# Sinkhorn attention followed by a squared-ReLU FFN: TensorE's order written out by hand, the first batch in halves, exp written contiguously

## The chip, the cores and the metric

The kernel runs on one core of one Trainium2 chip. The metric is the device time of one execution in microseconds (us); lower is better. Weights and activations arrive from device memory as float32 and are cast to bfloat16 by the loads; the result is stored as float32.

## The reference

Four batches, eight heads, 768 positions of width 64. A sorting matrix `P` (8 x 8 for each head) is made by five rounds of exp and row and column normalisation. It mixes the eight blocks (96 positions each) of `k` and `v`; each block of `q` then attends to the mixed block of the same number. The result, 3072 tokens of width 512, goes through a two-layer FFN.

```python
for _ in range(5):
    P = P - np.max(P, axis=-1, keepdims=True)
    P = np.exp(P)
    P = P / (np.sum(P, axis=-1, keepdims=True) + 1e-09)
    P = P / (np.sum(P, axis=-2, keepdims=True) + 1e-09)
k_sorted = np.einsum('bhij,bhjcd->bhicd', P, k_b).reshape(B, H, S, D)
v_sorted = np.einsum('bhij,bhjcd->bhicd', P, v_b).reshape(B, H, S, D)
...
scores = scale * np.matmul(q_b, k_sb.transpose(0, 1, 2, 4, 3))
attn = np.exp(scores)   # after subtraction of the row maximum
attn = attn / (np.sum(attn, axis=-1, keepdims=True) + 1e-09)
out = np.matmul(attn, v_sb)
...
h = np.maximum(x @ w_in, 0.0)      # 512 -> 2048
y = h * h @ w_out                  # 2048 -> 512
```

## The kernel before

The kernel is written against a layer that records operations, puts them in an order for each engine by its own priorities, and adds the semaphores. Every engine then executes its own instructions strictly in that order, so an instruction that waits holds up all behind it on its engine.

**Start.** `sort_net` is loaded on SP's queue; ScalarE and VectorE alternate through the five rounds (lines 90 to 112), and eight small matmuls (`pt`, line 117) and five VectorE products (`build_w`, line 127) spread the matrix over `w_all`. All loads of `q`, `k`, `v` and of the weights are issued by GpSimd (POOL, lines 72, 148, 151), which also fills the padding of the work tiles (`sT`, `et`, `vs`, lines 188, 194, 223). POOL is one queue: a fill that stands behind a load whose turn has not come waits with it.

**Attention** works on a pair of heads at a time: `attention(b, hp)`, four pairs in each batch, 16 in all. In order: 12 transposes of `q` (`qtp`, line 162) and a copy to `qT` on VectorE; 12 matmuls for `k` and 12 for `v` (`tp`, line 176), taken out by ScalarE (line 185) and by VectorE (line 187); 16 score matmuls (`scp`, line 200) and four exps on ScalarE (`et`, line 206); 8 transposes of `v` (`vbp`, line 215), copied by VectorE; 16 value matmuls (`oup`, line 231), normalised by VectorE (lines 238 and 239); 8 transposes back (`xtp`, line 247), copied to `xT` (line 251). The exp reads a row of scores contiguously from PSUM, ordered n, a, c, and writes it to `et` ordered n, c, a: neighbours that it reads land 12 bytes apart in SBUF.

**FFN**, `ffn_group(mc)`, works on 512 tokens, six groups in all: 16 steps of four matmuls of 512 columns (`hp`, line 258), each followed by a ReLU on ScalarE (line 264) and a square on VectorE (line 265); then four output tiles of 16 matmuls (`op`, line 270), a copy on ScalarE (line 276) and a store.

PSUM is shared out by pools: `ps1` has one slot (tag `p1`: `qtp`, `vbp`, `xtp`), `ps2` two (tag `p2`: `tp`, `scp`, `oup`), `psf` three (tag `pf`: `hp`, `op`). A slot is free again when its tile has been read out. The main loop runs batch 0's attention, then for each later batch its attention and one or two FFN groups of the batch before; which matmul of the two stands next on TensorE was the recording layer's choice.

Of the kernel before, what the change touches and what calls it, by code (L numbers as in the profile page):

```python
# [8 lines left out]
FP32 = mybir.dt.float32  # L9
# [7 lines left out]
def kernel(  # L17
# [18 lines left out]
    HP = H // 2  # L36
    d_model = moe_w_in.shape[0]
# [4 lines left out]
    MC = n_tok // 512  # L42
# [3 lines left out]
    sink = ctx.enter_context(tc.tile_pool(name="sink", bufs=1))  # L46
    wpool = ctx.enter_context(tc.tile_pool(name="wpool", bufs=1))
# [18 lines left out]
    def load(b, parts):
        n = H // parts
        ts = [ld.tile([128, H, NA * D], BF16, tag=t, name=t) for t in ("qb", "kb", "vb")]
        qkv[b] = ts
        for g in range(parts):  # L70
            for t, src in zip(ts, (q_r, k_r, v_r)):
                nc.gpsimd.dma_start(  # L72
                    out=t[:, n * g:n * (g + 1), :],
                    in_=src[b, :, n * g:n * (g + 1), :])

    ident = const.tile([128, 128], BF16)
    make_identity(nc, ident)
    load(0, 4)
# [34 lines left out]


    pt = ps1.tile([128, NB, NH], FP32, tag="p1")
    for i in range(NB):
        nc.tensor.matmul(
            out=pt[:, i, :],
            lhsT=pb[:, i, :, :].rearrange("h j c -> h (j c)"),
            rhs=ident[0:NH, 0:NH],  # L120
            start=True, stop=True)


    w_all = wpool.tile([128, NH, NB, C0], BF16)

    def build_w(h0, n):
        nc.vector.tensor_tensor(
            out=w_all[:, h0:h0 + n, :, :],
            in0=mask[:, None, None, :].to_broadcast([128, n, NB, C0]),
            in1=pt[:, :, h0:h0 + n].rearrange("p i h -> p h i")[:, :, :, None]  # L130
            .to_broadcast([128, n, NB, C0]),
            op=ALU.mult)

    build_w(0, 2)
    build_w(2, 6)
    for b in range(1, B):
        build_w(8 * b, 8)

    w_in_bf = wpool.tile([128, KC, d_ff], BF16)
    w_out_bf = wpool.tile([128, NT, d_model], BF16)  # L140
    xT = wpool.tile([128, KC, n_tok], BF16)
    w_in_r = moe_w_in.rearrange("(kc p) f -> p kc f", p=128)
    w_out_r = moe_w_out.rearrange("(nt p) m -> p nt m", p=128)

    def load_weights():
        for g in range(2):
            f = slice(d_ff // 2 * g, d_ff // 2 * (g + 1))
            nc.gpsimd.dma_start(out=w_in_bf[:, :, f], in_=w_in_r[:, :, f])
        for g in range(2):
            t = slice(NT // 2 * g, NT // 2 * (g + 1))  # L150
            nc.gpsimd.dma_start(out=w_out_bf[:, t, :], in_=w_out_r[:, t, :])

    def attention(b, hp):
        hA = 2 * hp
        qb, kb, vb = qkv[b]
        w = [w_all[:, 8 * b + hA + e, :, :].rearrange("p i c -> p (i c)") for e in range(2)]


        qtp = ps1.tile([128, NA, 128], BF16, tag="p1")
# [6 lines left out]
        qT = att.tile([128, NB, NA, C0], BF16, tag="qT")
        nc.vector.tensor_copy(  # L167
            out=qT, in_=qtp.rearrange("p a (i c) -> p i a c", c=C0))


        st = []
        for name, src, eng in (("ks", kb, "act"), ("vs", vb, "dve")):
            tp = ps2.tile([128, NA, 128], FP32, tag="p2")
            for a in range(NA):
                for e in range(2):
                    nc.tensor.matmul(  # L176
                        out=tp[64 * e:64 * (e + 1), a, :],
                        lhsT=src[:, hA + e, D * a:D * (a + 1)],
                        rhs=w[e], start=True, stop=True)

            sT = att.tile([128, S + 32], BF16, tag=name + "T")
            view = sT[:, 0:S].rearrange("p (i c a) -> p i c a", c=C0, a=NA)
            tpv = tp.rearrange("p a (i c) -> p i c a", c=C0)
            if eng == "act":
                nc.scalar.copy(out=view, in_=tpv)  # L185
            else:
                nc.vector.tensor_copy(out=view, in_=tpv)  # L187
            nc.gpsimd.memset(sT[:, S:S + 32], 0.0)  # L188
            st.append(sT)
        ksT, vsT = st  # L190


        et = att.tile([96, 2, S + 32], BF16, tag="et")
        nc.gpsimd.memset(et[:, :, S:S + 32], 0.0)  # L194
        for hf in range(2):
            scp = ps2.tile([128, 2, 512], FP32, tag="p2")
            for n in range(4):
                i = 4 * hf + n
# [54 lines left out]
    def ffn_group(mc):  # L253
# [70 lines left out]
```

## Time and profile before

| | us |
|---|---|
| median of 3 runs | 349.79 (349.43 to 349.99) |
| profiled execution, its own time | 349.75 |
| span of the profiled execution, first to last instruction | 348.0 |
| TensorE busy, matmuls | 260.1 |
| ScalarE busy | 168.1 |
| VectorE busy | 119.8 |
| mean granted TensorE clock (1.00 is 2.4 GHz) | 0.882 |

Some 1.75 us of a run lie outside the span. Busy times are unions over an engine's instructions; matmuls are pipelined and their ends are modelled, so the distance between the starts of two pieces of work says more than a matmul's own duration. Times below are counted from the span's start.

### The profile page before, as it was taken

To read this page: it belongs to the slowest core of one execution; us is meant where nothing else is said; L and a number is where in the kernel's file an instruction comes from. 1 tells how busy PE (TensorE), PEld (TensorE's weight loads), DVE (VectorE), ACT (ScalarE), POOL (GpSimd) and SP (SyncE) were. 2 spreads that over 40 slices of the span, in tenths; PEclk is the share of its full clock that TensorE was granted. 3 is DMA by queue.
4 is the path that set the end of the run, shared out by engine and by line. 5 is a ranking of instruction groups with operands and counts; after the bars stand their busy time and mean duration, and the time that the engine had idled before them with its cause. 6 is when DMAs were issued, how large, how long until landed. Compare 5 with 4: busy or idle time off the path is not lost.

```text
span 348.0 us, 5090 instructions
## 1 busy us (share of the span) xinstructions
PE 260.1 (75%) x2083; PEld 138.1 (40%) x2120; DVE 119.8 (34%) x260; ACT 168.1 (48%) x206; POOL 31.9 (9%) x104
## 2 busy tenths in 40 slices
PE   0224566569669598766969999966867899999995
PEld 0123344335335344433534444433534444444442
DVE  5812254246236302533531141143544303402400
ACT  2133643685673515577471362277476315514611
POOL 8812003200004100000000000000000000000000
PEclk9999965688686899888689999988678899999999
DMA  7999961940004931000001200200000021011011
GB/s 101 200 211 207 204 107 21 191 62 2 0 3 52 196 85 62 0 2 0 2 1 44 79 0 33 81 11 0 2 0 2 0 78 45 0 60 62 1 60 60
DMA packets 19430, 20.25 MB, mean 58 GB/s; under 512 B 976, under 2 KB 15312, under 8 KB 19408
## 3 DMA queue, kind: packets, MB, share of 16 engines
q0 software_dynamic: 15904, 13.63, 25.2%
q1 hardware_dynamic: 3504, 6.30, 4.8%
q8 instruction: 16, 0.26, 0.3%
q14 instruction: 6, 0.05, 0.1%
HBM read 27.27 MB, written 6.29 MB: 96 GB/s over the span
## 4 chain that ended last, share of the span: by engine, by line
PE 62%; ACT 21%; issue 8%; DMA 6%; POOL 1%; DVE 1%; ACTq 0%; POOLq 0%
PE op L270 24%; PE hp L258 23%; ACT et L206 17%; PE tp L176 6%; DMA w_in_bf<-in_moe_w_in_dram 4%; PE xtp L247 3%; PE qtp L162 2%; ACT h L264 2%; PE oup L231 2%; DMA kb<-in_k_dram 2%; DVE ao L239 1%; PE scp L200 1%; ACT sT L185 0%; POOL qb L72 0%; POOL vb L72 0%
## 5 line engine op out<-in xcount | busy, mean ns | idle before, releaser
L258 PE MATMUL hp<-xT,w_in_bf 128*128 128x512 bf16 x356 | 102.8, 419 | 3.7 <-issue 3.0
L206 ACT ACTIVATE et<-scp 96x384 bf16<-96x384 f32 x64 | 85.0, 1595 | 20.9 <-PE scp L200 20.8
L270 PE MATMUL op<-w_out_bf,h 128*128 128x512 bf16 x375 | 85.1, 382 | 0.6 <-issue 0.2
L264 ACT ACTIVATE h<-hp 128x512 bf16<-128x512 f32 x96 | 60.0, 627 | 49.1 <-PE hp L258 35.0
L265 DVE TENSOR_TENSOR h<-h 128x512 bf16<-128x512 bf16 x96 | 40.7, 424 | 77.7 <-ACT h L264 77.6
L231 PE MATMUL oup<-vs,et 96*128 96x65 bf16 x256 | 19.2, 220 | 51.7 <-ACT et L206 47.0
L270 PEld LDWEIGHTS <-h 128*128 128x128 bf16 x384 | 37.5, 99 | 44.6 <-issue 0.8
L258 PEld LDWEIGHTS <-w_in_bf 128*128 128x128 bf16 x384 | 36.9, 104 | 42.6 <-issue 11.2
L276 ACT COPY ob<-op 128x512 f32<-128x512 f32 x24 | 14.1, 586 | 71.6 <-PE op L270 68.7
L231 PEld LDWEIGHTS <-et 96*128 96x128 bf16 x256 | 13.3, 113 | 61.9 <-ACT et L206 55.9
L238 DVE RECIPROCAL rec<-oup 96x8 f32<-96x8 f32 x32 | 6.4, 199 | 59.1 <-PE oup L231 59.1
L185 ACT CAST sT<-tp 128x768 bf16<-128x768 f32 x16 | 12.8, 799 | 27.8 <-PE tp L176 27.8
L239 DVE TENSOR_TENSOR ao<-oup,rec 96x512 bf16<-96x512 f32 x32 | 21.9, 684 | 0.7
L194 POOL MEMSET et<- 96x64 bf16 x16 | 2.4, 151 | 195.5 <-PE oup L231 195.5
L247 PE MATMUL xtp<-ident,ao 96*128 96x96 bf16 x128 | 15.8, 270 | 2.7 <-DVE ao L239 2.3
L167 DVE COPY qT<-qtp 128x768 bf16<-128x768 bf16 x16 | 8.8, 552 | 25.2 <-PE qtp L162 25.2
L247 PEld LDWEIGHTS <-ao 96*128 96x128 bf16 x128 | 12.2, 132 | 13.3 <-issue 8.1
L220 DVE COPY vs<-vbp 96x1024 bf16<-96x1024 bf16 x16 | 11.0, 686 | 18.6 <-PE vbp L215 18.6
L187 DVE CAST sT<-tp 128x768 bf16<-128x768 f32 x16 | 15.3, 957 | 3.7 <-PE tp L176 3.7
L200 PE MATMUL scp<-qT,sT 64*128 64x96 bf16 x256 | 9.7, 217 | 9.0 <-POOL sT L188 8.0
L251 DVE COPY xT<-xtp 128x768 bf16<-128x768 bf16 x16 | 8.9, 558 | 21.2 <-PE xtp L247 21.2
L200 PEld LDWEIGHTS <-sT 64*128 64x128 bf16 x256 | 6.8, 101 | 18.1 <-issue 8.7
(34 smaller groups left out, 128.4 us busy)
## 6 DMA issues: line engine op xcount, KB each, us to landing
out_dram<-ob SPq DMA_DIRECT2D x24, 256.0 KB, 2.0
qb<-in_q_dram POOLq DMA_DIRECT2D x6, 384.0 KB, 9.0
kb<-in_k_dram POOLq DMA_DIRECT2D x6, 384.0 KB, 10.1
vb<-in_v_dram POOLq DMA_DIRECT2D x6, 384.0 KB, 11.3
w_in_bf<-in_moe_w_in_dram POOLq DMA_DIRECT2D x2, 1024.0 KB, 13.5
w_out_bf<-in_moe_w_out_dram POOLq DMA_DIRECT2D x2, 1024.0 KB, 21.6
qb<-in_q_dram POOLq DMA_DIRECT2D x4, 192.0 KB, 6.1
kb<-in_k_dram POOLq DMA_DIRECT2D x4, 192.0 KB, 6.4
```

Of the source, the lines that this page charges most:

```text
L176: nc.tensor.matmul(out=tp[64 * e:64 * (e + 1), a, :], lhsT=src[:, hA + e, D * a:D * (a + 1)], rhs=w[e], start=True, stop=True)
L187: nc.vector.tensor_copy(out=view, in_=tpv)
L200: nc.tensor.matmul(out=scp[:, e, BLK * n:BLK * (n + 1)], lhsT=ksT[64 * e:64 * (e + 1), BLK * i:BLK * i + 128], rhs=qT[64 * e:64 * (e + 1), ...
L206: nc.scalar.activation(out=et[:, e, 384 * hf:384 * (hf + 1)].rearrange("p (n c a) -> p n a c", c=C0, a=NA), in_=scp[0:96, e, 0:384].rearra ...
L231: nc.tensor.matmul(out=oup[:, e, 66 * n:66 * n + D + 1], lhsT=et[:, e, BLK * i:BLK * i + 128], rhs=vs[:, i, e, 0:D + 1], start=True, stop= ...
L239: nc.vector.tensor_tensor(out=ao[:, 4 * hf:4 * (hf + 1), :, :].rearrange("p n e d -> p e n d"), in0=ov[:, :, :, 0:D], in1=rec[:, :, :, Non ...
L247: nc.tensor.transpose(out=xtp[:, i, :], in_=ao[:, i, :, :].rearrange("p e d -> p (e d)"), identity=ident[0:96, 0:96])
L258: nc.tensor.matmul(out=hp, lhsT=w_in_bf[:, kc, 128 * nt:128 * (nt + 1)], rhs=xT[:, kc, 512 * mc:512 * (mc + 1)], start=(kc == 0), stop=(kc ...
L264: nc.scalar.activation(out=h1, in_=hp, func=AF.Relu)
L265: nc.vector.tensor_tensor(out=h2[:, nt, :], in0=h1, in1=h1, op=ALU.mult)
L270: nc.tensor.matmul(out=op, lhsT=h2[:, nt, 128 * mt:128 * (mt + 1)], rhs=w_out_bf[:, nt, :], start=(nt == 0), stop=(nt == NT - 1))
L276: nc.scalar.copy(out=ob, in_=op)
```

## The change

- **TensorE's order is fixed.** `tc.manual_schedule(engines={PE})` makes TensorE execute in the order in which the code is written; ScalarE and VectorE are still ordered by the recording layer. Attention is split into the pieces `s_q`, `sort_kv`, `s_sc`, `s_vt`, `s_av`, `s_xt` of a `Unit`, and the FFN into chunks of four matmuls; `lay` gives each piece the number of the chunk ahead of which it stands.
- **FFN groups** are of 384 tokens, eight in all: 16 chunks of four matmuls of 384 columns and 12 chunks of four of 512, 28 chunks a group. The columns in total are the same as before.
- **The first batch in halves.** The first half (positions 0 to 383) of all four pairs runs ahead of the FFN, the four `q` transposes ahead of the sorting matrix; the second half lies in FFN group 0, batch 1 in group 1, batch 2 in groups 2 and 3, batch 3 in groups 4 and 5; groups 6 and 7 are FFN alone.
- **exp** reads PSUM with a step (neighbours 64 bytes apart) and writes `et` contiguously. `late` puts the recording of each exp, and of each normalisation, behind the next chunk.
- **Padding** is filled once, by VectorE at the start, in three buffers each of `ksT`, `vsT`, `vs` and four of `et`. POOL then issues loads alone: batch 0's `q` first, `w_in` in four parts, half of batch 1 ahead of `w_out`.
- `build_w` for batches 1 to 3 is recorded in halves, from a bfloat16 copy `pt`.

```diff
+    for n in range(3):
+        for r, name in ((ksT_r, "ksT"), (vsT_r, "vsT")):
+            sT = const.tile([128, 2, HS + 32], BF16, name=f"{name}{n}")
+            nc.vector.memset(sT[:, :, HS:HS + 32], 0.0)
...
-            for e in range(2):
-                nc.scalar.activation(
-                    out=et[:, e, 384 * hf:384 * (hf + 1)].rearrange(
-                        "p (n c a) -> p n a c", c=C0, a=NA),
-                    in_=scp[0:96, e, 0:384].rearrange("p (n a c) -> p n a c", c=C0, a=NA),
-                    func=AF.Exp, scale=scale)
+            def ex(e, scp=scp, et=u.et[hf]):
+                nc.scalar.activation(
+                    out=et[:, e, 0:HS].rearrange("p (n c a) -> p n c a", c=C0, a=NA),
+                    in_=scp[0:96, e, 0:HS].rearrange("p (n a c) -> p n c a", c=C0, a=NA),
+                    func=AF.Exp, scale=scale)
+            for e in range(2):
+                late.append(lambda e=e, ex=ex: ex(e))
...
-            nc.scalar.activation(out=h1, in_=hp, func=AF.Relu)
+            h1 = ffn.tile([128, HS], BF16, tag="h1", name="h1", bufs=3)
+            nc.scalar.activation(out=h1, in_=hp[:, 0:HS], func=AF.Relu)
...
+    ctx.enter_context(tc.manual_schedule(engines={mybir.EngineType.PE}))
+    for hp in range(HP):
+        s_q(0, hp, "act")
...
+    us = [Unit(0, hp, (0,)) for hp in range(HP)]
+    for n in range(HP + 3):
+        if n < HP:
+            s_sort(us[n], 1)
+            s_sort(us[n], 2)
+        if 0 <= n - 1 < HP:
+            s_sc(us[n - 1])
+            flush()
+            s_vt(us[n - 1])
+        if 0 <= n - 2 < HP:
+            s_av(us[n - 2])
+            flush()
+        if 0 <= n - 3 < HP:
+            s_xt(us[n - 3])
...
+    def lay(us, c0, c1, first):
+        step = (c1 - c0) / (len(us) + 0.8)
+        for n, u in enumerate(us):
+            c = c0 + step * n
+            put(c + step * 0.0, sort_kv, u)
+            put(c + step * 0.35, s_sc, u)
+            put(c + step * 0.5, s_vt, u)
+            put(c + step * 0.75, s_av, u)
+            put(c + step * 1.2, s_xt, u)
+
+    lay([Unit(0, hp, (1,)) for hp in range(HP)], 0, n_up, True)
+    first = [n_up, 2 * n_up, 4 * n_up, 6 * n_up]
+    for b in range(1, B):
+        put(max(first[b - 1] - 12, 2), build_w, H * b, HP, pt)
+        put(max(first[b - 1] - 8, 2), build_w, H * b + HP, HP, pt)
+        lay([Unit(b, hp, (0, 1)) for hp in range(HP)], first[b - 1], first[b], False)
...
+    chunks = [f for g in range(n_tok // HS) for f in ffn_chunks(g)]
+    for c, f in enumerate(chunks):
+        for g in at.get(c, []):
+            g()
+        f()
+        if late:
+            late.pop(0)()
```

The next rows are POOL's queue in the kernel before, from the last loads of batch 1 on: the first fills of the work tiles stand behind them.

```order
L72 DMA qb<-in_q_dram 128x4x384 [waits DMASW3_49]
L72 DMA kb<-in_k_dram 128x4x384 [waits DMASW4_49]
L72 DMA vb<-in_v_dram 128x4x384 [waits DMASW5_49]
L188 MEMSET sT 128x32 x2
L194 MEMSET et 96x2x32
L223 MEMSET vs 96x16
```

In the changed kernel the fills are VectorE's first rows, ahead of the first step of the sorting matrix (`rs`), and no engine queue has a load ahead of them.

```order
L107 MEMSET vsT_130 128x2x16
L110 MEMSET vs_132 96x16
L114 MEMSET et_134 96x2x16
L114 MEMSET et_136 96x2x16
L114 MEMSET et_138 96x2x16
L114 MEMSET et_140 96x2x16
L311 TENSOR_REDUCE rs<-p_sb 32x8 [waits Activation_49]
```

On ScalarE, one pair of heads of batch 2 in the kernel before, from the take-out of `k` (`sT`) to the next one: two ReLUs (`h`), four exps, two ReLUs.

```order
L185 CAST sT<-tp 128x768 [waits PE_49,Pool_49]
L264 ACTIVATE h_1848<-hp 128x512 [waits DVE_49,PE_49]
L264 ACTIVATE h_1856<-hp 128x512 [waits DVE_49,PE_49]
L206 ACTIVATE et<-scp 96x4x6x16 [waits PE_49]
L206 ACTIVATE et<-scp 96x4x6x16
L206 ACTIVATE et<-scp 96x4x6x16 [waits PE_49]
L206 ACTIVATE et<-scp 96x4x6x16
L264 ACTIVATE h_1864<-hp 128x512 [waits DVE_49,PE_49]
L264 ACTIVATE h_1872<-hp 128x512 [waits DVE_49,PE_49]
L185 CAST sT<-tp 128x768 [waits PE_49,Pool_49]
```

The same engine in the changed kernel, the first pair of batch 1: the exps have an unstepped output row of 384, and stand between the ReLUs of chunks that TensorE runs while they work.

```order
L184 CAST ksT_128<-tp 128x2x384 [waits PE_49]
L277 ACTIVATE h_1010<-hp 128x384 [waits DVE_49,PE_49]
L277 ACTIVATE h_1027<-hp 128x384 [waits DVE_49,PE_49]
L203 ACTIVATE et_134<-scp 96x384 [waits PE_49]
L203 ACTIVATE et_134<-scp 96x384
L203 ACTIVATE et_136<-scp 96x384 [waits PE_49]
L203 ACTIVATE et_136<-scp 96x384
L277 ACTIVATE h_1063<-hp 128x384 [waits DVE_49,PE_49]
L277 ACTIVATE h_1072<-hp 128x384 [waits DVE_49,PE_49]
L277 ACTIVATE h_1102<-hp 128x384 [waits DVE_49,PE_49]
L184 CAST ksT_116<-tp 128x2x384 [waits PE_49]
```

VectorE in the changed kernel, at the turn from the first to the second pair of batch 1: the normalisations of the first pair (`rec`, `ao`) stand ahead of the second pair's `qT` and of the take-out of its `v` (`vsT`).

```order
L220 COPY vs_132<-vbp 96x16x64 [waits PE_49]
L278 TENSOR_TENSOR h_1004<-h_1063 128x384 [waits Activation_49]
L240 RECIPROCAL rec<-oup 96x8 [waits PE_49]
L278 TENSOR_TENSOR h_1004<-h_1072 128x384 [waits Activation_49]
L241 TENSOR_TENSOR ao<-oup,rec 96x2x4x64 [waits DVE_49]
L240 RECIPROCAL rec<-oup 96x8 [waits PE_49]
L241 TENSOR_TENSOR ao<-oup,rec 96x2x4x64 [waits DVE_49]
L278 TENSOR_TENSOR h_1004<-h_1102 128x384 [waits Activation_49]
L164 COPY qT<-qtp 128x768 [waits PE_49]
L186 CAST vsT_118<-tp 128x2x384 [waits PE_49]
```

In the kernel before, the same turn on VectorE (two pairs of batch 1) has the same work, with the copy to `xT` ahead of the next pair's `sT` and `qT`; in the changed kernel that copy comes behind them.

```order
L238 RECIPROCAL rec<-oup 96x8 [waits PE_49]
L265 TENSOR_TENSOR h_1128<-h_1190 128x512 [waits Activation_49]
L239 TENSOR_TENSOR ao<-oup,rec 96x2x4x64 [waits DVE_49]
L238 RECIPROCAL rec<-oup 96x8 [waits PE_49]
L239 TENSOR_TENSOR ao<-oup,rec 96x2x4x64 [waits DVE_49]
L265 TENSOR_TENSOR h_1128<-h_1198 128x512 [waits Activation_49]
L251 COPY xT<-xtp 128x768 [waits PE_49]
L187 CAST sT<-tp 128x768 [waits PE_49,Pool_49]
L167 COPY qT<-qtp 128x768 [waits PE_49]
```

TensorE's rows show the order that `lay` writes: in batch 1, `qtp`, `tp`, `tp`, 8 matmuls of FFN, `scp`, `vbp`, 8 of FFN, `oup`, 4 of FFN, the next pair's `qtp`, `tp`, `tp`, 8 of FFN, and then `xtp` of the first pair. In batches 2 and 3 there are about twice as many FFN matmuls in each gap.

## Rows read from the trace of the kernel before

**Rows 1.** The page's busy times, share of the span and instructions of each engine.
```profile
PE 260.1 (75%) x2083; PEld 138.1 (40%) x2120; DVE 119.8 (34%) x260; ACT 168.1 (48%) x206; POOL 31.9 (9%) x104
```
**Rows 2.** Stretch, us; busy us of PE, PEld, DVE, ACT, POOL; clock, DMA, GB/s.
```profile
62.00:71.00 9.00, 4.81 (x64) 3.53 (x63) 3.53 (x7) 5.29 (x5) 1.22 (x8) 0.69 1.28 192
...
112.00:133.00 21.00, 17.44 (x113) 8.54 (x107) 3.62 (x8) 7.71 (x9) 2.63 (x10) 0.92 0.77 137
133.00:182.00 49.00, 35.11 (x389) 19.88 (x396) 22.19 (x46) 32.77 (x36) 1.49 (x16) 0.83 0.02 7
...
274.00:316.00 42.00, 41.79 (x198) 19.21 (x200) 7.87 (x19) 14.25 (x24) 0.00 (x0) 1.00 0.12 44
```
**Rows 3.** Waits: engine, line, releaser: us in total, times, longest.
```profile
PE oup L231 <- ACT et L206: 47.0, 42, 2.2
```
**Rows 4.** Timeline, one pair of heads in batch 2: start, us, instruction, [idle before].
```profile
144.37 0.53 PE L176 MATMUL tp<-w_all,kb 128*64 128x128 bf16 x12
144.83 0.39 PE L258 MATMUL hp<-xT,w_in_bf 128*128 128x512 bf16 x1
145.06 0.34 PE L247 MATMUL xtp<-ident,ao 96*128 96x96 bf16 x4
145.32 0.53 PE L176 MATMUL tp<-w_all,vb 128*64 128x128 bf16 x12
...
146.10 0.53 PE L162 MATMUL qtp<-ident,qb 128*64 128x128 bf16 x12
146.56 1.25 PE L258 MATMUL hp<-xT,w_in_bf 128*128 128x512 bf16 x4
147.74 0.52 PE L200 MATMUL scp<-qT,sT 64*128 64x96 bf16 x16
148.13 5.28 ACT L206 ACTIVATE et<-scp 96x384 bf16<-96x384 f32 x4
148.19 0.62 PE L215 MATMUL vbp<-ident,sT 128*128 128x128 bf16 x8
148.65 1.03 PE L258 MATMUL hp<-xT,w_in_bf 128*128 128x512 bf16 x4
150.91 0.36 PE L231 MATMUL oup<-vs,et 96*128 96x65 bf16 x6 [1.24 <-ACT et L206]
152.19 0.20 PE L231 MATMUL oup<-vs,et 96*128 96x65 bf16 x1 [0.92 <-ACT et L206]
153.47 0.46 PE L231 MATMUL oup<-vs,et 96*128 96x65 bf16 x9 [1.07 <-ACT et L206]
153.76 0.60 PE L258 MATMUL hp<-xT,w_in_bf 128*128 128x512 bf16 x2
```
**Rows 5.** Groups by line on ScalarE: busy us, mean ns of one, idle before.
```profile
L276 ACT COPY ob<-op 128x512 f32<-128x512 f32 x24 | 14.1, 586 | 71.6 <-PE op L270 68.7 <-remote 2.9
...
L185 ACT CAST sT<-tp 128x768 bf16<-128x768 f32 x16 | 12.8, 799 | 27.8 <-PE tp L176 27.8
```
**Rows 6.** The chain that ended last: start, us, engine and line.
```profile
196.54 4.96 PE hp L258 x23
...
343.99 0.59 ACT ob L276
```
**Rows 7.** Timeline of the start.
```profile
12.23 0.39 PE L117 MATMUL pt<-ident,pb 32*128 32x32 bf16 x8 [12.23 <-DVE pb L108]
...
12.65 4.68 DVE L127 TENSOR_TENSOR w_all<-mask,pt 128x256 bf16<-128x256 bf16 x5 [0.48 <-PE pt L117]
...
13.13 0.85 PE L176 MATMUL tp<-w_all,kb 128*64 128x128 bf16 x12 [0.51 <-DVE w_all L127]
...
27.64 0.74 POOL L72 DMA_DIRECT2D vb<-in_v_dram  x1 [4.19 <-DMA w_in_bf<-in_moe_w_in_dram]
...
28.57 0.26 PE L200 MATMUL scp<-qT,sT 64*128 64x96 bf16 x2 [7.99 <-POOL sT L188]
```
**Rows 8.** What the DMA engines moved in 40 slices of 8.7 us, written bytes.
```profile
GB/s 101 200 211 207 204 107 21 191 62 2 0 3 52 196 85 62 0 2 0 2 1 44 79 0 33 81 11 0 2 0 2 0 78 45 0 60 62 1 60 60
```

More of the change, by code (lines that the diff above doesn't have):

```diff
@@ L64, with alloc_qkv @@
     qkv = {}
[L66 to L74, printed above, removed]
+    def alloc_qkv(b):
+        qkv[b] = [ld.tile([128, H, NA * D], BF16, tag=t, name=t) for t in ("qb", "kb", "vb")]
@@ L76, with load @@
+    def load(b, t, h0, n):
+        nc.gpsimd.dma_start(
+            out=qkv[b][t][:, h0:h0 + n, :],
+            in_=(q_r, k_r, v_r)[t][b, :, h0:h0 + n, :])
+    alloc_qkv(0)
+    load(0, 0, 0, 2)
     ident = const.tile([128, 128], BF16)
     make_identity(nc, ident)
-    load(0, 4)
+    load(0, 0, 2, 2)
+    load(0, 0, 4, 4)
+    for g in range(4):
+        load(0, 1, 2 * g, 2)
+        load(0, 2, 2 * g, 2)
+    for g in range(4):
+        f = slice(d_ff // 4 * g, d_ff // 4 * (g + 1))
+        nc.gpsimd.dma_start(out=w_in_bf[:, :, f], in_=w_in_r[:, :, f])
@@ L115 @@
[L115 to L159, printed above, removed]
+    class Unit:
+        count = 0
+        ets = 0
+        def __init__(self, b, hp, halves):
+            self.b, self.hp, self.halves = b, hp, halves
+            n = Unit.count % 3
+            Unit.count += 1
+            self.ksT, self.vsT, self.vs = ksT_r[n], vsT_r[n], vs_r[n]
+            self.et = {}
+            for hf in halves:
+                self.et[hf] = et_r[Unit.ets % 4]
+                Unit.ets += 1
+            self.i0, self.ni = NQ * halves[0], NQ * len(halves)
@@ L163, in attention @@
                     out=qtp[64 * e:64 * (e + 1), a, :],
-                    in_=qb[:, hA + e, D * a:D * (a + 1)],
+                    in_=qb[:, 2 * hp + e, D * a:D * (a + 1)],
                     identity=ident)
[L166 to L174, printed above, removed]
-                for e in range(2):
[L176 to L198, printed above, removed]
+        qT = att.tile([128, NB, NA, C0], BF16, tag="qT", name="qT", bufs=5)
+        qTs[b, hp] = qT
+        src = qtp.rearrange("p a (i c) -> p i a c", c=C0)
+        if eng == "act":
+            nc.scalar.copy(out=qT, in_=src)
+        else:
+            nc.vector.tensor_copy(out=qT, in_=src)
@@ L199, in attention, with s_sc @@
+    def s_sc(u):
+        qT = qTs[u.b, u.hp]
+        for hf in u.halves:
+            scp = ps2.tile([128, 2, 512], FP32, tag="p2", name="scp")
+            for n in range(NQ):
                 for e in range(2):
@@ new lines, with build_w @@
+    pt_ps = psf.tile([128, NB, NH], FP32, tag="pf", name="pt_ps")
+    for i in range(NB):
+        nc.tensor.matmul(
+            out=pt_ps[:, i, :],
+            lhsT=pb[:, i, :, :].rearrange("h j c -> h (j c)"),
+            rhs=ident[0:NH, 0:NH],
+            start=True, stop=True)
+    pt = const.tile([128, NB, NH], BF16)
+    def build_w(h0, n, src):
+        nc.vector.tensor_tensor(
+            out=w_all[:, h0:h0 + n, :, :],
+            in0=mask[:, None, None, :].to_broadcast([128, n, NB, C0]),
+            in1=src[:, :, h0:h0 + n].rearrange("p i h -> p h i")[:, :, :, None]
+            .to_broadcast([128, n, NB, C0]),
+            op=ALU.mult)
```

251 lines of the change are left out of this document (161 added, 90 removed).

## The prediction

> **What bounds the kernel now.** I read the totals first, then stretches, then one pair of heads. TensorE is busy for 260 of 348 us and no other engine comes near [rows 1], but its share changes with the stage. Where the FFN runs alone it is busy without a break at the full clock, 41.79 of 42 us at 1.00 (2.4 GHz); where attention and FFN alternate it is busy for 35.11 of 49 us at a granted clock of 0.83 [rows 2]. The waits say for what: `oup` waits for the exps, 47.0 us in 42 waits [rows 3]. One pair of heads shows how: the scores start at 147.74, the four exps run one behind the other for 5.28 us from 148.13, and TensorE has only `vbp` and four FFN matmuls to fill that time, so that it waits 1.24, 0.92 and 1.07 us for one exp after the other, 3.2 us in all [rows 4]. The first batch has no FFN beside it at all: attention starts at 13.13, and its first pair is held up for 8 us more by a fill on POOL that stands behind loads which wait for `w_in` [rows 7]. So the kernel is bound by order, and in attention by ScalarE's exps; FFN at the end is bound by TensorE.
>
> **The exps.** Four take 5.28 us, 1.32 each, for 384 elements of each partition [rows 4]. The contiguous copy of 512 from PSUM takes 0.586, and the take-out of `k`, 768 elements, 0.799 [rows 5]. Between them lie 0.83 ns an element, so 384 cost 0.49 us. Is exp itself slow, or its stepped write? The trace has no exp of that size with a contiguous write. Bounds: 0.49 and the present 1.32. I take 0.49, because the change keeps what line 185 has, a stepped read (512 bytes from neighbour to neighbour) and a contiguous write, and line 185 is fast; that leaves the stepped write as what sets the present exp apart, or the function. Over 64 exps it takes 53 of ScalarE's 168 us, but none of this is a term of the sum: it counts where TensorE waits.
>
> The Trainium skill speaks against it: "Advanced Engine Details and Errata", section "Memory Cachelines", says that PSUM has lines of 8 bytes, that a non-contiguous pattern slows matmuls, and that every two neighbours should be contiguous for the best throughput. Taken as a rule for ScalarE's reads too, a step of 64 bytes would keep each exp slow, and the time would be that of the second rival below. Line 185 steps by 512 bytes and pays nothing that I can see, so in this trace the row disagrees with the rule as far as ScalarE's reads go.
>
> **The sum.** With TensorE's order fixed, the time is: when the FFN starts, plus all that TensorE does from there, plus its waits, plus the tail.
>
> - *FFN's start, 31 us.* The `q` transposes now stand ahead of `pt` on TensorE, and share one `p1` slot. A pair costs 0.85 at the low clock (12 small matmuls, [rows 7]), a copy on ScalarE of 0.8 [rows 5] and two hand-overs, some 1.85 in all. ScalarE takes the first copy behind four of the five exps of the sorting matrix, near 8 us (an estimate: five rounds end at 12.23 with `pt` [rows 7]); so the last transposes end near 13.9, and `pt` comes there in place of 12.23. All of `q` has landed by 8.7 us (0.79 MB, the first slice moves 0.88 [rows 8]). Then 16 tiles (`k`, `v`, scores, values, four half pairs) pass through two `p2` slots, each holding one for matmuls of 0.4, an evacuation of 0.5 to 0.9 and 0.3 of hand-overs: 1.4 x 16 / 2 = 11. The last half pair's normalisation, transposes and copy add 2. `build_w` for the other batches now lies between VectorE's evacuations: 24 of the 32 heads of 4.68 us [rows 7] are 3.5, of which I count 2. 14.8 + 11.2 + 2 + 2 = 30, and 1 for fills on VectorE ahead of the sorting matrix and the 5th exp behind a copy. Bounds: 28 (only the slots count) and 35 (as 20 tiles, nothing hidden).
> - *FFN, 165.6 us.* 23 matmuls of 512 columns in 4.96 us are 0.2157 each [rows 6]: 384 of them, 82.8; and 512 of 384 columns, at three quarters, 82.8. Bound above: 384 columns cost as much as 512, 27.6 more. At 2.4 GHz 0.2157 us are 518 cycles, nearly all columns, so I take the proportion.
> - *Attention's matmuls, 46.2 us.* From start to start at the full clock: `tp` 0.46 twice, `xtp` 0.26 for four, `qtp` 0.46, `scp` 0.45, `vbp` 0.46, `oup` 0.29 for nine [rows 4]. A pair: 0.92 + 0.52 + 0.46 + 0.45 + 0.46 + 0.52 = 3.3. Twelve whole pairs 39.6, four half pairs 6.6.
> - *Switches, 6 us.* Five FFN matmuls from 146.56 to 147.74 take 0.10 more than five times 0.2157, others 0.01 to 0.10 [rows 4]; five switches for each of 16 units, 0.08 each. Bounds 0 and 8.
> - *Waits, 8 us.* Batch 1 is the tightest: `lay` gives a pair 28 / 4.8 = 5.8 chunks. From the scores to `oup` lie 0.46 + 8 x 0.162 = 1.75; four exps need 0.3 + 4 x 0.49 = 2.25, two of them 1.3: the second half of `oup` waits 0.25. Behind it, the next pair's `v` needs the slot that VectorE's normalisations free: five instructions at a mean of 0.48 (22.19 / 46 [rows 2]) and 0.2, against 0.65 + 0.92 of TensorE's own work, 0.5 to 1.0 late. VectorE holds `qT` and the take-out of `v` behind them, and `scp` waits for both. I take 0.8 for each of these four pairs and 0.4 for the other twelve, where the gaps are wider or the tiles half. Bounds 0 and the present 3.2 for a pair, 51.
> - *Clock, 3 us.* The first half batch runs at 1.2 GHz like the present start; the FFN's first matmuls do too until it rises.
> - *Tail, 4 us:* from the last copy, 343.99, to the end of the span, 348.0 [rows 6]; it stays.
>
> 31 + 165.6 + 46.2 + 6 + 8 + 3 + 4 = 263.8, and 1.75 outside the span: 265.5 us. The same sum stands against the profiled execution (348.0 + 1.75 = 349.75), which is the median within 0.04.
>
> What is free and by what cover: the ReLUs, 128 in place of 96, 0.49 each, lie under chunks of 0.65; VectorE has 5.5 us for a pair [rows 2] under some 8 of TensorE. POOL's fills go to VectorE at the start, ahead of a load of `sort_net` that it waits for anyway. Loads: batch 0 and `w_in` (4.46 MB) are there at 26 us, `w_out` after half of batch 1 (7.74 MB) at 42 [rows 8]; its first matmul comes at about 47. Without those 5 us the FFN would wait, microsecond for microsecond.
>
> **The rivals.**
>
> 1. *The clock does not hold.* TensorE keeps making short stops at hand-overs, and the interleaved work, 124.2 + 46.2 + 6 = 176 us, gets the 0.83 that the same mix has now [rows 2]: 36 us more, 301; at the 0.92 of 112 to 133, 15 more, 281. For it: every interleaved stretch now is under 1.00. Against it: those have stops of a microsecond and more in each pair, which this order fills. The Trainium skill has a rule for it, "TensorE: Matmul & The Clock Gate", section "A second HAM failure mode: psum-queue depth-cycling": small idle times between groups that cycle through PSUM make the clock swing. In the pure FFN stretch the trace disagrees (groups of four in three slots, 1.00); for the mix it may hold.
> 2. *The exp stays at 1.32.* Then `oup` waits 3.6 for each pair of batch 1, 2.4 for those of batches 2 and 3, 1.2 for a half pair, and the first half batch takes 7 more: 14 + 19 + 5 + 7 = 45, so 311. ScalarE's row at line 185 is against it.
> 3. *384 columns cost like 512:* 293.
> 4. *Slower than before.* The clock again, as one mechanism at the places where FFN and attention alternate: the loss of 84 us that undoes the gain needs 176 / c = 260, a mean granted clock of 0.68. The stretch from 62 to 71 has 0.69 [rows 2], with TensorE busy for half the time and no FFN to fill it. At the low level throughout it would be 441.
>
> That the change doesn't do what it says is hardly a case for TensorE: its rows stand in the written order.
>
> **How the numbers follow.** A measurement of this kernel tells some 0.2% from no change. The sum with its own bounds (250 to 280: start 28 to 35, waits 3 to 16, switches 3 to 8) has 0.65; the clock 0.15, from 281 to 301; exp slow 0.08; the columns 0.06; below 250, 0.02; slower 0.03, no change 0.01. The range from 250 to 296 holds the first, the third rival and half of the clock's, some 0.78.
>
> **What would show it.** Exps of about 0.5 us and hardly a wait of `oup` for them; FFN's first matmul at 28 to 35; the granted clock near 1.00 from there; no wait on POOL; the gap between neighbouring `hp` matmuls 0.162. Wrong if the clock in the mix is 0.9 or less, if the waits come back as `scp` or `v` waiting for VectorE by more than 1 us a pair, or if `w_out` is late.

## The result, and the profile after

The changed kernel takes 249.78 us (median of 4 runs, 248.82 to 250.25) against 349.61 for the one before, a ratio of 0.7145 (95% interval 0.7117 to 0.7173). The forecast was 265.5 with a range of 250 to 296: the direction is right, and so are the exps, the FFN and the clock; the size is off by 15.7 us, most of it in the price of attention, and the time lies 0.2 us under the range. The profiled execution took 249.91 us with a span of 248.1, so 1.8 us lie outside.

The page's busy times and the granted clock in 40 slices, after:

```profile
PE 229.1 (92%) x2344; PEld 136.8 (55%) x2344; DVE 123.5 (50%) x317; ACT 119.1 (48%) x247; POOL 26.7 (11%) x41
...
PEclk9999999999999999999999999999999999999999
```

Beside [rows 1] TensorE is busy for 31 us less although it has 224 weight loads more, each with a matmul, and ScalarE for 49 us less. The columns of the FFN are as many as before: most of TensorE's saving is the clock, 0.882 on average before. The row gives 9 in every slice now, but it can't be taken at its word for the first five: twelve transposes take 0.85 us at 12.04 and 0.53 at 65.40 (both shown below), so the start still runs at half pace.

The windows of the changed kernel (columns as in [rows 2]), cut where the FFN starts and at the starts of batch 1, batch 2, batch 3 and the FFN alone, up to the last matmul:

```profile
29.33:59.41 30.08, 29.24 (x281) 16.03 (x282) 14.10 (x36) 13.53 (x30) 4.45 (x6) 1.00 1.28 208
59.41:94.78 35.37, 34.35 (x450) 21.18 (x449) 21.75 (x48) 18.48 (x39) 4.46 (x6) 1.00 0.50 87
94.78:148.66 53.88, 53.88 (x562) 32.06 (x561) 27.46 (x64) 27.88 (x58) 0.00 (x0) 1.00 0.16 45
148.66:202.60 53.94, 53.94 (x562) 32.22 (x562) 27.47 (x64) 27.88 (x58) 0.00 (x0) 1.00 0.09 31
202.60:244.10 41.50, 41.50 (x225) 21.72 (x222) 11.47 (x32) 19.25 (x38) 0.00 (x0) 1.00 0.11 39
```

Where attention and FFN alternated at a clock of 0.83 [rows 2], TensorE now has no idle time at all in batches 2 and 3. The first number of each row is what the terms of the prediction are held against below.

TensorE's waits from 25 us to the end (engine, line, releaser: us in total, times, longest):

```profile
PE tp L173 <- DVE ao L241: 1.3, 4, 0.4
PE xtp L253 <- DVE xT L258: 0.9, 2, 0.6
PE oup L231 <- DVE vs L220: 0.2, 1, 0.2
```

The 47.0 us for which `oup` waited for the exps [rows 3] have no row any more. The two waits of `xtp` lie ahead of the FFN; of those of `tp`, two lie in the half pairs of group 0 and two in batch 1. The groups on ScalarE (busy us, mean ns, idle before), which answer to [rows 5]:

```profile
L277 ACT ACTIVATE h<-hp 128x384 bf16<-128x384 f32 x128 | 63.0, 493 | 30.4 <-PE hp L271 29.4
...
L203 ACT ACTIVATE et<-scp 96x384 bf16<-96x384 f32 x64 | 27.4, 489 | 14.1 <-PE scp L195 14.0
```

An exp of 384 elements takes 0.489 us, as a ReLU of the same size does. The first pair of batch 1, and the turn to the second, in the timeline, which answers to [rows 4]:

```profile
61.94 0.51 PE L195 MATMUL scp<-qT,ksT 64*128 64x96 bf16 x16
...
62.43 1.62 ACT L203 ACTIVATE et<-scp 96x384 bf16<-96x384 f32 x4
...
62.84 1.46 PE L271 MATMUL hp<-xT,w_in_bf 128*128 128x384 bf16 x8
...
64.14 0.67 PE L231 MATMUL oup<-vs,et 96*128 96x65 bf16 x16
...
65.14 0.68 DVE L241 TENSOR_TENSOR ao<-oup,rec 96x512 bf16<-96x512 f32 x1
65.40 0.53 PE L154 MATMUL qtp<-ident,qb 128*64 128x128 bf16 x12
...
65.88 0.53 PE L173 MATMUL tp<-w_all,kb 128*64 128x128 bf16 x12
65.97 0.69 DVE L241 TENSOR_TENSOR ao<-oup,rec 96x512 bf16<-96x512 f32 x1
...
66.71 0.53 PE L173 MATMUL tp<-w_all,vb 128*64 128x128 bf16 x12 [0.31 <-DVE ao L241]
```

Four exps run in 1.62 us in place of 5.28, and all 16 value matmuls follow without a stop at 64.14. What is left here is the wait of the next pair's `v` for VectorE's second normalisation, 0.31 us. Batch 2, where the gaps are wider, has no such wait; its first pair begins so:

```profile
94.78 0.53 PE L154 MATMUL qtp<-ident,qb 128*64 128x128 bf16 x12
95.14 0.50 PE L173 MATMUL tp<-w_all,kb 128*64 128x128 bf16 x12
95.47 0.50 PE L173 MATMUL tp<-w_all,vb 128*64 128x128 bf16 x12
95.91 2.77 PE L271 MATMUL hp<-xT,w_in_bf 128*128 128x384 bf16 x16
```

The start, which answers to [rows 7]; the last row is the FFN's first matmul:

```profile
12.04 0.85 PE L154 MATMUL qtp<-ident,qb 128*64 128x128 bf16 x12 [0.89 <-ACT qT L162]
...
12.82 0.39 PE L336 MATMUL pt_ps<-ident,pb 32*128 32x32 bf16 x8
...
13.72 0.54 PE L173 MATMUL tp<-w_all,kb 128*64 128x64 bf16 x12 [0.51 <-DVE w_all L345]
...
28.48 0.53 PE L173 MATMUL tp<-w_all,kb 128*64 128x64 bf16 x12
...
29.26 2.74 PE L271 MATMUL hp<-xT,w_in_bf 128*128 128x384 bf16 x8
```

The `q` transposes make `pt` late by 0.6 us beside [rows 7], not by the 1.7 that were forecast, and no work of TensorE, ScalarE or VectorE waits on POOL. The row at 28.48 is already the second half of the first pair, whose `k` and `v` stand ahead of the FFN. The long pieces at the end of the chain that ended last, which answer to [rows 6] (the chain counts the FFN's first matmul from 29.33, where the one before it ends):

```profile
29.33 2.67 PE hp L271 x8
...
202.60 10.40 PE hp L271 x64
213.00 10.36 PE op L285 x48
```

64 matmuls of 384 columns take 10.40 us, 0.1625 each; 48 of 512 take 10.36, 0.2158 each: three quarters, as the sum had it. The `w_out` loads and the stores make no row among the waits [rows 8].

### The profile page after: what moved, and what is told of

Its sections match the earlier page's. It is cut to its first block, busy times and chain, and to the rows that moved or that the text cites. A ratio compares the mean times of both kernels' runs of the same rounds, so it can differ in the third digit from the quotient of the medians.

```text
span 248.1 us, 5559 instructions
## 1 busy us (share of the span) xinstructions
PE 229.1 (92%) x2344; PEld 136.8 (55%) x2344; DVE 123.5 (50%) x317; ACT 119.1 (48%) x247; POOL 26.7 (11%) x41
## 4 chain that ended last, share of the span: by engine, by line
PE 84%; DVE 8%; ACT 4%; issue 1%; DMA 1%
PE op L285 33%; PE hp L271 33%; PE tp L173 5%; PE vbp L216 3%; PE scp L195 3%; DVE ao L241 3%; PE qtp L154 3%; PE oup L231 2%; PE xtp L253 2%; ACT h L277 1%; DVE h L278 1%; DVE vs L220 1%; DVE w_all L345 1%; DMA p_sb<-in_sort_net_dram 1%; ACT qT L162 1%
## 5 line engine op out<-in xcount | busy, mean ns | idle before, releaser
L271 PE MATMUL hp<-xT,w_in_bf 128*128 128x384 bf16 x512 | 93.9, 330 | 0.0
L277 ACT ACTIVATE h<-hp 128x384 bf16<-128x384 f32 x128 | 63.0, 493 | 30.4 <-PE hp L271 29.4
L278 DVE TENSOR_TENSOR h<-h 128x384 bf16<-128x384 bf16 x128 | 45.2, 355 | 58.8 <-ACT h L277 57.7
L271 PEld LDWEIGHTS <-w_in_bf 128*128 128x128 bf16 x512 | 47.2, 99 | 29.7 <-issue 1.4
L285 PEld LDWEIGHTS <-h 128*128 128x128 bf16 x384 | 35.9, 98 | 39.2
L203 ACT ACTIVATE et<-scp 96x384 bf16<-96x384 f32 x64 | 27.4, 489 | 14.1 <-PE scp L195 14.0
L184 ACT CAST ksT<-tp 128x768 bf16<-128x768 f32 (+1 forms) x20 | 13.4, 671 | 17.7 <-PE tp L173 17.6
L186 DVE CAST vsT<-tp 128x768 bf16<-128x768 f32 (+1 forms) x20 | 15.9, 794 | 2.2 <-PE tp L173 1.7
L220 DVE COPY vs<-vbp 96x1024 bf16<-96x1024 bf16 (+1 forms) x20 | 11.6, 578 | 6.8 <-PE vbp L216 6.2
L173 PE MATMUL tp<-w_all,vb 128*64 128x128 bf16 (+1 forms) x240 | 9.9, 222 | 2.7 <-DVE ao L241 1.3
L216 PE MATMUL vbp<-ident,vsT 128*128 128x128 bf16 x128 | 11.5, 233 | 0.3 <-DVE xT L258 0.3
```

Source lines behind the costliest of these rows:

```text
L173: nc.tensor.matmul(out=tp[64 * e:64 * (e + 1), a, :], lhsT=src[:, 2 * u.hp + e, D * a:D * (a + 1)], rhs=w_all[:, H * u.b + 2 * u.hp + e, u ...
L186: nc.vector.tensor_copy(out=dst, in_=tpv)
L203: nc.scalar.activation(out=et[:, e, 0:HS].rearrange("p (n c a) -> p n c a", c=C0, a=NA), in_=scp[0:96, e, 0:HS].rearrange("p (n a c) -> p ...
L216: nc.tensor.transpose(out=vbp[:, n, :], in_=u.vsT[:, i // NQ, BLK * (i % NQ):BLK * (i % NQ) + 128], identity=ident)
L271: nc.tensor.matmul(out=hp[:, 0:HS], lhsT=w_in_bf[:, kc, 128 * nt:128 * (nt + 1)], rhs=xT[:, kc, t0:t0 + HS], start=(kc == 0), stop=(kc == ...
L277: nc.scalar.activation(out=h1, in_=hp[:, 0:HS], func=AF.Relu)
```

## Experiments

Each time is a median with its ratio to the kernel before on the same chip. "After" is the changed kernel, 249.78.

**1. The exp alone.** The kernel before, with the exp's two patterns exchanged and nothing else.

```diff
-                        "p (n c a) -> p n a c", c=C0, a=NA),
-                    in_=scp[0:96, e, 0:384].rearrange("p (n a c) -> p n a c", c=C0, a=NA),
+                        "p (n c a) -> p n c a", c=C0, a=NA),
+                    in_=scp[0:96, e, 0:384].rearrange("p (n a c) -> p n c a", c=C0, a=NA),
```

> The kernel before with nothing changed but the exp's access patterns: stepped read, contiguous write. Theory (both are needed: a fast exp shortens the chain, the new order fills what is left): the exp falls to 0.49 us each, some 3.2 us of waiting for each of 16 pairs go, 51 us, and the clock in the mix rises, for 10 to 15 us more: about 285 us, 278 to 300. Rival A (the exp alone is the gain): 260 or less. Rival B (the order alone is the gain, the exp was hidden anyway): above 330.

272.52 us, ratio 0.779 (0.7758 to 0.7822): lower than the theory had it. The page's group of the exp, and its granted clock (POOL's hold of the scores is left, and shown in experiment 3):

```profile
L206 ACT ACTIVATE et<-scp 96x384 bf16<-96x384 f32 x64 | 26.3, 487 | 21.5 <-PE scp L200 21.5
...
PEclk9999998959999999999999999999999999999998
```

One line brings 77 of the 100 us. The theory had 51 us for the waits and 10 to 15 for the clock. Measured, TensorE's idle time in the span fell by 48, from 87.9 to 39.7, and its busy time by 29, from 260.1 [rows 1] to 230.8, with the mean clock, which rose from 0.882 to 0.977: the clock's part was twice the theory's. Here a wait that comes back in every pair was paid for a second time, in the clock of the work around it.

**2. Everything but the exp.** The changed kernel with the exp's patterns as before: contiguous read, stepped write.

```diff
-                    out=et[:, e, 0:HS].rearrange("p (n c a) -> p n c a", c=C0, a=NA),
-                    in_=scp[0:96, e, 0:HS].rearrange("p (n a c) -> p n c a", c=C0, a=NA),
+                    out=et[:, e, 0:HS].rearrange("p (n c a) -> p n a c", c=C0, a=NA),
+                    in_=scp[0:96, e, 0:HS].rearrange("p (n a c) -> p n a c", c=C0, a=NA),
```

> The changed kernel with the exp as before: contiguous read, stepped write, 1.32 us each. Theory (both are needed): waits of the value matmuls for the exps come back, 2.4 to 3.6 us a pair, and the first half batch is longer: 285 to 300 us. Rival A (exp alone): 330 or more. Rival B (the order hides the exps whatever they cost): 255 or less.

296.31 us, ratio 0.8461 (0.8429 to 0.8492), 46.5 more than after; the second rival had priced this at 45. The exp's group in the kernel before and in this one, and three of TensorE's waits:

```profile
L206 ACT ACTIVATE et<-scp 96x384 bf16<-96x384 f32 x64 | 85.0, 1595 | 20.9 <-PE scp L200 20.8
...
L203 ACT ACTIVATE et<-scp 96x384 bf16<-96x384 f32 x64 | 86.6, 1570 | 13.9 <-PE scp L195 13.8
```
```profile
PE oup L231 <- ACT et L203: 9.8, 9, 2.1
PE hp L271 <- ACT h L277: 7.4, 4, 1.9
...
PE hp L271 <- ACT ob L292: 5.8, 2, 2.9
```

Same function, same size, same place in the program: 1.570 us with the stepped write, 0.489 with the stepped read. The edit exchanges read and write together, but a contiguous read can't be what is slow: the copy of 512 elements reads contiguously in 0.586 [rows 5]. So it is the stepped write. (These are an instruction's own times, and neighbours overlap: by the groups' busy time an exp comes every 1.33 us before and every 0.43 after, 27.4 / 64.) The waits show where it hurts: no longer only `oup`, but the FFN's `hp` too, which waits for ReLUs and copies on ScalarE; that these queue behind the slow exps and hold the `pf` slots is the likely reason. That the rival's 45 came so near is in part luck: 38 of it were waits of `oup` for the exps, which take 9.8. Measured against after, TensorE is idle for 36 us more and busy for 10 more (239.2), at a mean clock of 0.969.

**3. The exp and the fills.** The kernel before with the exp of experiment 1, and its three kinds of fills on VectorE (still in every pair).

```diff
-            nc.gpsimd.memset(sT[:, S:S + 32], 0.0)
+            nc.vector.memset(sT[:, S:S + 32], 0.0)
...
-        nc.gpsimd.memset(et[:, :, S:S + 32], 0.0)
+        nc.vector.memset(et[:, :, S:S + 32], 0.0)
...
-        nc.gpsimd.memset(vs[:, :, :, D:D + 1], 1.0)
+        nc.vector.memset(vs[:, :, :, D:D + 1], 1.0)
```

> The kernel before with two parts of the change alone: exp written contiguously, and the padding filled by VectorE instead of POOL. Theory: the hold of 7.8 us on the first fill, still in the trace with the exp alone (272.5 us), lies on the path and goes: 264 to 267 us. Rival: behind the fill stands another hold, of loads or of VectorE, now laden with fills in each pair, and it stays at 270 to 274. If order in pieces and halves were worth nothing beside these two, 250; I expect some 15 us to be left for it.

263.12 us, ratio 0.7547 (0.7518 to 0.7576): 9.4 less than with the exp alone (8.5 by the two ratios), just under the theory's 264 to 267. The first pair's scores, in experiment 1 and here:

```profile
28.50 0.26 PE L200 MATMUL scp<-qT,sT 64*128 64x96 bf16 x2 [7.80 <-POOL sT L188]
```
```profile
19.05 0.82 PE L200 MATMUL scp<-qT,sT 64*128 64x96 bf16 x16 [0.65 <-DVE sT L188]
```

The hold is gone, and the gain is no shorter than it was: it lay on the path. So two small edits to the old kernel give 86 of the 100 us, and all else that the change does (pieces, halves, groups of 384, order of the loads, fixed order) together the last 13.

**4. No fixed order.** The changed kernel, its pieces recorded in the same order, but TensorE ordered by the recording layer like the other engines.

```diff
-    ctx.enter_context(tc.manual_schedule(engines={mybir.EngineType.PE}))
```

> The changed kernel without the line that fixes TensorE's order: the recording layer orders it, from the same code in pieces. In its rows the FFN's chunks move by a few matmuls and a first half pair's last piece moves behind the next one's sorting; from batch 2 on they hardly differ. Theory (what matters is that the code is written in pieces with room between them): within 2 us of the changed kernel, 248 to 252. Rival (fixing the order is what keeps TensorE from waiting): 256 or more.

246.01 us, ratio 0.7032 (0.6989 to 0.7076): faster than after, and the fastest kernel of this study. So fixing the order gains nothing here; what of the last 13 us the pieces, the groups of 384 and the order of the loads give each was not taken apart. TensorE in its start, and where batches 1 and 2 begin:

```profile
23.36 0.61 PE L216 MATMUL vbp<-ident,vsT 128*128 128x128 bf16 x4
23.76 1.17 PE L271 MATMUL hp<-xT,w_in_bf 128*128 128x384 bf16 x3
24.72 0.65 PE L231 MATMUL oup<-vs,et 96*128 96x65 bf16 x8
...
57.97 0.53 PE L154 MATMUL qtp<-ident,qb 128*64 128x128 bf16 x12
...
92.80 0.53 PE L154 MATMUL qtp<-ident,qb 128*64 128x128 bf16 x12
```

The first three FFN matmuls, which need no more of `xT` than the first pair's part (one matmul of each of three chunks), stand 5.5 us earlier than after, between the pieces of the last half pairs. The hand order keeps a chunk's four matmuls together and puts all of them behind the fourth pair. Batch 1 begins 1.4 us earlier than after (57.97 against 59.41) and batch 2 2.0 (92.80 against 94.78), and the traced execution, 247.92, is 2.0 shorter: 1.4 are gained ahead of batch 1, 0.5 in it, and nothing behind it. The traced execution is the longest of the four; where the shorter ones gain more, no trace shows.

**5. Where the free order gains.** Order free up to the tenth FFN chunk, fixed from there.

```diff
-    ctx.enter_context(tc.manual_schedule(engines={mybir.EngineType.PE}))
...
     for c, f in enumerate(chunks):
+        if c == 10:
+            ctx.enter_context(tc.manual_schedule(engines={mybir.EngineType.PE}))
```

> The changed kernel with TensorE's order left to the recording layer up to the tenth chunk of the FFN, and fixed by hand from there. Theory: what the free order of the whole kernel gained, 246.0 against 249.8 us, is gained in the first 35 us, where it sets the sorting matrix's matmuls ahead of the last transposes of q and the first FFN matmuls between the last half pairs: 245 to 247.5. Rival: it is gained by finer steps between attention and FFN later on, and then this kernel stays at 249 to 250.5.

247.07 us, ratio 0.7082 (0.705 to 0.7114), within the theory's range: by the medians the start gives 2.7 of the 3.8 us. Where batch 1 begins:

```profile
57.54 0.53 PE L154 MATMUL qtp<-ident,qb 128*64 128x128 bf16 x12
```

That is 1.9 us before after's 59.41, and all by which the traced execution, 248.03, is shorter. The intervals of experiments 4 and 5 overlap, and their traced executions differ by 0.1, so whether the free order gains more than its start stays open.

**6. No halves.** The changed kernel with all of batch 0 ahead of the FFN, and none of it in group 0.

```diff
-    us = [Unit(0, hp, (0,)) for hp in range(HP)]
+    us = [Unit(0, hp, (0, 1)) for hp in range(HP)]
...
-    lay([Unit(0, hp, (1,)) for hp in range(HP)], 0, n_up, True)
```

> The changed kernel with the first batch whole, ahead of the FFN, and no attention beside FFN group 0. Theory: the FFN starts some 14 us later, at 43, and group 0 takes 20.7 in place of 30.1, so that 4 to 6 us are lost: 254 to 256 us. Rival (the halves buy nothing, since TensorE does the same work in either order): within 1 us of the changed kernel.

252.18 us, ratio 0.7205 (0.7176 to 0.7234): 2.4 more, less than expected (and only 0.8 more in the span of the profiled execution, 248.9). The windows ahead of the FFN's first matmul, at 37.8 us, and from there to 59.4, where group 0 ends in the changed kernel:

```profile
29.30:37.80 8.50, 6.81 (x91) 5.77 (x89) 6.41 (x16) 1.62 (x4) 2.30 (x4) 0.50 1.27 205
37.80:59.40 21.60, 21.55 (x111) 11.15 (x110) 6.30 (x17) 9.01 (x18) 2.22 (x3) 0.93 1.29 209
```

The FFN starts 8.5 us later, at the low clock, but group 0 then runs without attention in it and is over at 60.2 in place of 59.4. The halves move attention's work more than they hide it.

**7. Attention's whole price.** The changed kernel without the pieces of batches 1 to 3.

```diff
-                    rhs=xT[:, kc, t0:t0 + HS],
+                    rhs=xT[:, kc, t0 % S:t0 % S + HS],
...
-        lay([Unit(b, hp, (0, 1)) for hp in range(HP)], first[b - 1], first[b], False)
```

> The changed kernel without the attention of batches 1 to 3: no piece of their twelve pairs is issued, and their FFN groups read the result of batch 0 again, so the columns of the FFN are the same. The measured pitches after the change say that the twelve pairs with all their switches and waits cost 39.4 us, so 249.8 - 39.4 = 210.4 us (209 to 212). The prediction's separate terms, 39.6 of matmuls, 4.8 of switches and 6.4 of waits for these pairs, say 199 (197 to 201).

210.6 us, ratio 0.6031 (0.6009 to 0.6053): 39.2 us less than after, the price of twelve pairs. The measured pitches said 39.4, the prediction's terms 50.8.

**8. Narrower gaps.** Batches 2 and 3 in 28 chunks each, like batch 1.

```diff
-        lay([Unit(b, hp, (0, 1)) for hp in range(HP)], first[b - 1], first[b], False)
+        lay([Unit(b, hp, (0, 1)) for hp in range(HP)], first[b - 1], first[b - 1] + n_up, False)
```

> Batches 2 and 3 each laid into 28 chunks of the FFN instead of 56, as batch 1 already is; nothing else differs. If half the gaps still cover the exps and normalisations, as batch 1's pairs without a recorded wait say, nothing is lost: 249 to 251 us. By the prediction's waits, 0.8 us instead of 0.4 for eight pairs, it is 253; if the pairs of batch 1 were spared only by chance and each tight pair waits as much as before the change (3.2 us), 270 or more.

254.47 us, ratio 0.7289 (0.7261 to 0.7317), 4.7 more than after. "Nothing is lost" has fallen; the prediction's 253 was closer. A tight pair of batch 2 in the timeline:

```profile
100.69 0.53 PE L154 MATMUL qtp<-ident,qb 128*64 128x128 bf16 x12
101.16 0.53 PE L173 MATMUL tp<-w_all,kb 128*64 128x128 bf16 x12
102.00 0.53 PE L173 MATMUL tp<-w_all,vb 128*64 128x128 bf16 x12 [0.31 <-DVE ao L241]
```

From the start of `k` to that of `v` are 0.84 us, against 0.33 in a wide pair (95.14 to 95.47 after): `v` needs the `p2` slot that the pair before it still holds. Batch 1 has the same after, 0.83 or 0.84 in two of its pairs and 0.55 in a third. Its four pairs take 35.37 - 20.76 = 14.6 us beside their FFN group, those of batches 2 and 3 12.4 each. A tight batch costs 2.2 us more, 0.56 a pair, and two of them 4.4 of the 4.7 measured.

**9 and 10. `v` one chunk later.** Experiment 8's kernel, and then experiment 5's, with `tp` of `v` moved from right behind that of `k` to the next chunk.

```diff
         s_sort(u, 1)
+
+    def sort_v(u):
         s_sort(u, 2)
...
             put(c + step * 0.0, sort_kv, u)
+            put(c + step * 0.15, sort_v, u)
```

> The dense kernel (batches 2 and 3 in 28 chunks each, 254.5 us) with one thing moved: in a pair's piece the matmuls for v stand one FFN chunk behind those for k. Theory: a tight pair loses 0.57 us, 0.31 of it where v waits for the slot that VectorE's normalisation of the pair before frees, and a chunk of 0.65 covers that: nine pairs by 0.31 to 0.57, so 250 to 251.7 us. Rival: the wait only moves to the scores or to the second half of the values, since v is then taken out later, and it stays at 253.5 to 255.

> The kernel whose order is free up to the tenth chunk and fixed from there (247.1 us, span 246.2), with v one chunk behind k as in the dense one. Only batch 1 is tight here: three or four pairs by 0.31 to 0.57, so 245 to 246.5 us and a span of 244.2 to 245.3. If the wait only moves, 246.5 to 247.5 and a span of 246.

253.16 us, ratio 0.7239 (0.7209 to 0.7269), and 247.32, ratio 0.709 (0.7058 to 0.7121): a gain of 1.3 whose interval overlaps that of experiment 8, and none beside experiment 5. The theory has fallen; the rivals, by which the wait only moves (253.5 to 255, and 246.5 to 247.5), are near. The dense kernel's timeline:

```profile
102.05 0.53 PE L173 MATMUL tp<-w_all,vb 128*64 128x128 bf16 x12
...
103.16 0.51 PE L253 MATMUL xtp<-ident,ao 96*128 96x96 bf16 x8
103.60 0.70 PE L195 MATMUL scp<-qT,ksT 64*128 64x96 bf16 x16
```

`v` no longer waits, but the scores now take 0.63 us from start to start in place of 0.45 (103.60 to 104.23): the pause stands ahead of their second tile, which needs the slot of `v`, and VectorE reads `v` out until 103.90. With six tiles a pair through two slots, this tight pair pays somewhere else. A third `p2` slot wasn't tried.

## Why the prediction was right in kind and wrong in size

Measured from the windows above, with the 20.76 us of each FFN group (10.40 + 10.36) taken off the stretches (the pairs' terms are the prediction's own, its switches and waits split over the units; 80 switches of 0.08 are 6.4, of which its sum took 6):

| term | predicted | measured |
|---|---|---|
| start of the FFN | 31 | 29.3 |
| FFN | 165.6 | 166.1 |
| four half pairs: matmuls, switches, waits | 6.6 + 1.6 + 1.6 = 9.8 | 7.9 |
| batch 1 | 13.2 + 1.6 + 3.2 = 18.0 | 14.6 |
| batches 2 and 3 | 26.4 + 3.2 + 3.2 = 32.8 | 24.8 |
| clock after the start | 3 | 1.4 in the first eight matmuls |
| tail, and outside the span | 4 + 1.75 | 4.0 + 1.8 |

The start holds 0.8 us that belong to the half pairs (`k` and `v` from 28.48), and the half pairs' 7.9 hold 0.7 of waits; the sum is the same either way.

- *The exps* fell to 0.49 us, as forecast. (The prediction's 1.32 for the old ones is the distance from one to the next; the instruction's own time was 1.595.) Experiment 2 shows that the stepped write was slow. That the Trainium skill's "Advanced Engine Details and Errata", section "Memory Cachelines", asks for neighbours to be contiguous in PSUM changes nothing for ScalarE's reads here: 0.489 us with a step of 64 bytes. Rival 2 is out; experiment 2 met its price, but in part by other waits than it named.
- *FFN* was right within 0.5 us; rival 3 is out by 0.1625 us for 384 columns.
- *The clock* held at 1.00 in the mix; rivals 1 and 4 are out. The swing of which "TensorE: Matmul & The Clock Gate", section "A second HAM failure mode: psum-queue depth-cycling", of the Trainium skill warns does not show in the mix either. Of the 3 us, at least 1.4 are real: the eight matmuls that start at 29.33 take 2.67 us in place of 1.30. The pieces right behind them are slow too (the first two FFN matmuls from 32.77 still start 0.32 apart, the later ones 0.16), and lie in the 7.9.
- **The step that failed is attention's price: matmuls 46.2, switches 6, waits 8.** Of the 15.7 us, 12 to 13 are here. First, *switches* were counted twice: the pitches of [rows 4] run from the start of one piece to the start of the next, so what a switch out of a piece costs is in them. What is not in them is 0.09 us in the FFN's matmuls ahead of `qtp` and 0.10 ahead of `scp`, and 0.01 or nothing ahead of the others: 0.2 a pair in place of 0.4. Second, *waits* of 0.4 for the wide pairs are nothing: from 94.78 to 202.60 TensorE has no idle time. For the tight pairs the mechanism was the one named, the `p2` slot behind VectorE's normalisations, at 0.56 in place of 0.8. Third, the pitches themselves were long. The pieces of a wide pair now follow at 0.36 for `qtp`, 0.33 and 0.44 for `tp`, 0.45 for `scp`, 0.45 for `vbp`, 0.51 for `oup` and 0.34 for `xtp`, 2.9 us in place of 3.3; with the 0.2 a pair costs 3.1. Experiment 7 confirms the sum, 39.2. Why they were long follows below the list.
- *The start* came 1.7 us early: `k`'s first matmul stands at 13.72 and not 14.8, since the transposes delay `pt` by 0.6 and not 1.7, and what lies from there to the FFN takes 15.6 in place of 16.2.
- *The range* failed by its own working: its steps gave 0 as the lower bound of waits and of switches, and 28 for the start, which together reach 248.5; the range took 3 and 3 instead, which with 28 make 254.5, went down to 250 without naming a term for it, and called a time below that a chance of 0.02.

The clock is not why the pitches were long: in the stretch of the kernel before from which the pitches were read (columns as in [rows 2]) it was full.

```profile
144.37:153.76 9.39, 6.11 (x91) 3.66 (x92) 3.45 (x7) 7.53 (x8) 0.00 (x0) 1.00 0.01 2
```

The reason is what stands behind a piece. In [rows 4] FFN matmuls follow on `qtp` and on both `tp`, and each takes 0.46. In a wide pair after, `tp` follows on `qtp` and on the first `tp`, 0.36 and 0.33, and only the second, with FFN behind it, takes 0.44. Experiment 9 has both cases for `k`: 0.34 us where `v` follows at once (94.72 to 95.06), and 0.43 where the FFN does:

```profile
116.57 0.50 PE L173 MATMUL tp<-w_all,kb 128*64 128x128 bf16 x12
117.00 1.04 PE L285 MATMUL op<-w_out_bf,h 128*128 128x512 bf16 x4
```

`xtp` was two pieces of 0.26 and is now one of 0.34. So the new order made the pieces cheaper, and the prediction took their price from the old one.

What stays open: what the groups of 384, the pieces and the order of the loads give one by one, and the last 1.1 us of the free order. The 0.48 of `qtp` at 65.40, against 0.36 at 59.41, is no open end: its own matmuls are no slower, but `k` behind it needs the slot that the normalisation from 65.14 holds for 0.68 us, to 65.82.

## What to carry to other kernels

Price an instruction in a loop by its access pattern as well as by its size: compare it with a row of the same size on the same engine, and if it is three times as long, exchange the patterns before rebuilding the order around it (one line gave 77 of 100 us here). Read distances from start to start as they are, add no switches to them, but ask whether the new order puts the same neighbours behind each piece; and let the range reach the bounds that each step has itself. Try code in small pieces with the layer's own order before fixing it by hand: here the layer's order was the faster one.

## What the runs showed of the hardware

- ScalarE writing 2-byte elements 12 bytes apart in SBUF takes 1.570 us for 384 elements of each partition; reading float32 64 bytes apart from PSUM and writing contiguously 0.489, no more than a contiguous ReLU (0.493).
- Waits of a microsecond in every pair went with a lower clock of the work around them: with the exp alone changed, the mean clock went from 0.882 to 0.977 and TensorE's busy time down by 29 us. Two waits of 0.31 us in batch 1, and one of 0.23, left it at 1.00.
- Twelve matmuls of 128*64 weights and 128 columns take 0.33 to 0.36 us at the full clock where another twelve follow, and 0.43 to 0.46 where matmuls of 128*128 weights follow.
